# Even and odd tokens are put in order at y's eviction in two pieces per row instead of in the product, with a new order of all operations

## The chip, the cores and the metric

The kernel runs on 1 core of one Trainium2 chip. The metric is device time in microseconds; the time before is 193.65 us, the median of 3 runs (193.57 to 194.23). The core has five engines with a queue of instructions each: TensorE (PE in the profile; its weight loads are PEld), VectorE (DVE), ScalarE (ACT), GpSimd (POOL) and SyncE (SP). Here POOL and SP also issue nearly all the DMAs. Engines run their own queue in order and wait for each other by semaphores.

## What is computed

A gated linear recurrence for each of 4 batches and 8 heads, over 768 tokens with head size 48, and behind it a bilinear feed-forward over the 3072 tokens:

```python
state = np.zeros((B, H, D, D))                      # B, H, S, D = 4, 8, 768, 48
for t in range(S):
    state = alpha[:, :, t, :, None] * state + einsum('bhd,bhe->bhde', k[:, :, t], v[:, :, t])
    y[:, :, t] = einsum('bhd,bhde->bhe', q[:, :, t], state)
x = y.transpose(0, 2, 1, 3).reshape(B * S, H * D)   # 3072 x 384
out = ((x @ w_a) * (x @ w_b)) @ w_out               # 384 -> 1536 -> 384
```

Inputs and output are float32.

## The kernel before

**Chunks.** The work is cut into six chunks of 512 tokens: chunk c takes batches 0 and 1 (c even) or 2 and 3 (c odd), and of each of the two (called u = 0, 1, a "row") 256 tokens. A partition holds two neighbouring tokens, an even and an odd one (r = 0, 1), so all 256 tokens of a row are on 128 partitions, and each row falls into two halves of 128 tokens (g = 0, 1; partitions 0 to 63 and 64 to 127).

**An order written out by hand.** All operations stand in one string, `PROGRAM`. Each line begins with a chunk's number; then come operations with their arguments, separated by semicolons. They are called in this order, and each engine gets its instructions in that order; nothing is reordered later. A bank (0 to 7) in the arguments names the part of PSUM that an operation writes, a letter its engine: V for VectorE, S for ScalarE, P for GpSimd, Y for SyncE. The table OPS at the end maps names to functions. Those that matter here:

- `ld x u e` loads a, k, q or v (alpha, keys, queries, values) of a chunk; 0a and 0b are the two halves of the heads of u = 0. `W` and `Wo` load weights (POOL). They are DMAs, and POOL or SP spends about 0.5 to 1 us on issuing each.
- `c1a` calls for ScalarE's function table that has both the logarithm and the exponential. `cu`, `cus`, `ci`, `cm`, `cz`, `cs` and the like make constants; `fill` multiplies zeros.
- `ln` (la, line 556) takes the logarithm of alpha on ScalarE; `B`, `A2`, `AQ` sum it over tokens on TensorE; `ra` and `E` take exponentials on ScalarE.
- `mq` and `mk` (line 678) multiply q and k by these on VectorE into QKp; `C` transposes on TensorE and `Ce` evicts into kqT, or `T` transposes by DMA. `lv` prepares q and k of later chunks.
- `v` copies values into vx. `K`, `K2` and `k` carry the state over (Sm, S); `dk` and `de`, or `dr` and `dl`, bring its decay.
- `D` makes the scores on TensorE (line 841), masked by `M` (VectorE, line 846) or by `Mc` and `Mm` (ScalarE's copy, then VectorE in place).
- `SB`, `SA` and `Y` sum the row's output y in two banks of PSUM (line 865): 384 features in three groups of 128 partitions, for both halves g, 128 columns each, in which the 64 even tokens stand first and the 64 odd ones after them.
- `X u e` (`evac`, lines 900 and 902) evicts one row, 768 columns, into xT, the right-hand side of the feed-forward.
- `a` and `b` (`ff`, line 919) are the two first products of the feed-forward: for one of 12 groups f of 128 hidden features, three matmuls over the 384 inputs, for one row (0 or 1, 256 columns) or both (`*`, 512 columns). `as` (`ff_as`, line 925) evicts a on ScalarE, and `pr` (`ff_prod`, line 933) multiplies it on VectorE with b, which is still in PSUM, into prod.
- `o` and `oc` (lines 941 and 952) multiply prod by w_out, for 128 tokens m, in two halves of six groups; `ot`, `otc` evict and `st`, `stc` store.

**Where the even and odd tokens meet.** In xT each group of 128 tokens has the even ones first. `ff_prod` writes prod in token order: it reads a and b as (half, r, s) and writes every second element.

**How stages interleave.** The feed-forward of a chunk runs between the recurrence work of the next one. Chunk 0 has no other work to run beside it.

Of the kernel before, what the change touches and what calls it, by code (L numbers as in the profile page):

```python
# [50 lines left out]
1: ra 1
0: as 11 *
1: lv 0 q V; E 0 i
0: as 0 1; b 6 * 0; b 11 * 3; a 8 * 4; pr 6 *; pr 11 *
2: ld a * P
0: b 0 1 1; as 8 *; a 3 1 6
1: E 0 b; lv 0 k V
0: a 10 * 2; pr 0 1
1: mq 0 V; ld v 1 P
0: b 8 * 4  # L60
1: A2 1 7
0: as 10 *; b 10 * 2; pr 8 *
1: E 1 b
0: as 3 1; as 7 *; b 9 * 3; b 3 1 0; b 7 * 1; a 9 * 6
2: ld q * P
1: v 0 S; lv 1 q V; mk 0 V
0: pr 10 *
1: mq 1 V; C 0 1 4
0: as 9 *
1: C 0 0 2  # L70
0: o 0 0 5; pr 7 *
1: dk * 6
2: ld k * P
3: ld v * P
0: cz 1 v P; pr 9 *
1: Ce 0 0 S; E 1 i; de *; lv 1 k P; Ce 0 1 V; D 0 1 1; D 0 0 3
0: pr 3 1
1: Mc 0 0; K2 0 0 7 0
0: o 1 0 6
1: mk 1 V; M 0 1  # L80
0: o 3 0 4; o 1 1 -; ot 1 S; c3 P
3: ld a * P
0: cs 1 0 P; o 3 1 -
1: k 0 0 V; k 0 1 V; Mm 0 0 V; SB 0 1; C 1 0 3; C 1 1 7
0: ot 3 S; o 0 1 -
1: Ce 1 0 V
2: ln *
1: v 1 V; D 1 0 3; Ce 1 1 S; K2 1 1 6 0; Y 0; SA 0
0: ot 0 V
1: k 1 0 V; D 1 1 6  # L90
0: o 2 0 5
1: M 1 0
2: l2 0 V
1: X 0 S; a 3 0 1; Mc 1 1
2: l2s 0 P; l2s 1 P
1: a 2 0 3; a 4 0 4
2: R 0
1: k 1 1 V; as 4 0
2: ra 1
1: as 3 0; b 4 0 7  # L100
0: o 2 1 -
1: as 2 0
0: ot 2 S
1: pr 4 0
2: R 1; lv 1 q P
1: b 3 0 6; b 2 0 7; a 5 0 2; pr 3 0; b 5 0 3; as 5 0; b 1 0 5; a 1 0 1; pr 5 0; pr 2 0; a 7 0 2; as 1 0; pr 1 0
2: AQ 3
1: SB 1 6
2: lv 0 k P
1: a 10 0 5  # L110
2: lv 1 k V; ra 0; ld v * P
1: Mm 1 1 V
2: E 1 b
1: as 10 0; b 10 0 0; pr 10 0
2: mq 1 V; E 1 i
1: as 7 0; b 7 0 1
2: E 0 b; E 0 i
1: a 0 0 5
0: st 3 Y
2: dr  # L120
1: SA 1; Y 1
2: mk 1 V
1: pr 7 0; a 11 0 0; a 6 0 3; b 6 0 2; X 1 S; b 11 0 4; a 2 1 6; as 6 0; a 3 1 7; as 11 0; b 2 1 1; pr 6 0
2: lv 0 q V
1: b 4 1 0; as 2 1
2: T 1
1: pr 11 0
2: dl
0: st 0 Y
1: a 0 1 2; pr 2 1  # L130
2: mq 0 V
1: b 3 1 3; b 0 0 6; as 3 1; as 0 0; b 0 1 7; pr 3 1; a 8 0 1; a 9 0 5
0: st 1 Y
1: b 8 0 3; b 9 0 4; pr 0 0; as 0 1
2: mk 0 V
1: a 4 1 2
3: ln *
1: a 9 1 6; pr 0 1; as 8 0; b 9 1 1
3: ra 1
1: b 10 1 7; pr 8 0; a 10 1 3; as 4 1; as 9 0; as 9 1; a 6 1 6; b 6 1 2; b 11 1 5; pr 4 1; as 10 1; pr 9 0; a 11 1 4; pr 10 1; pr 9 1; as 6 1  # L140
2: v 1 S
1: a 8 1 3; b 8 1 1; a 7 1 6; pr 6 1
# [48 lines left out]
2: a 0 * 0; b 0 * 1; as 0 *; as 1 *
3: lv 0 k P; lv 0 q P
2: a 5 * 7
1: st 3 Y
2: a 7 * 4
4: l2s 1 P
2: a 2 * 5
3: lv 1 q V; mq 1 V; lv 1 k V
2: pr 1 *
3: dr  # L200
2: pr 0 *
3: mk 0 V
4: ld q * Y
0: st 2 Y
2: as 5 *; a 6 * 6; b 6 * 2; as 7 *
3: mq 0 V
2: b 9 * 4; b 7 * 0
1: st 2 Y
3: dl
4: R 0  # L210
2: b 5 * 7
1: o 1 0 3
2: a 9 * 1; pr 7 *; as 6 *
3: T 0
2: pr 6 *
4: ra 0
2: pr 5 *; a 11 * 6
3: mk 1 V
2: as 9 *; a 3 * 0
4: lv 0 k V; lv 0 q V; R 1  # L220
2: as 2 *
1: o 1 1 -
2: as 11 *; a 8 * 5; b 11 * 2; a 4 * 7; b 2 * 1
3: T 1
1: ot 1 V
2: pr 9 *; as 8 *; pr 11 *; pr 2 *; b 8 * 3; b 4 * 5; as 4 *
5: ld a * Y
3: K2 * * 4 6
2: pr 8 *; as 3 *; pr 4 *
3: k * 0 V; D 0 0 2; Mc 0 0  # L230
2: b 3 * 1
4: ra 1
2: pr 3 *; b 10 * 5; a 10 * 0
3: D 1 0 1; D 1 1 3
2: as 10 *
3: k * 1 V; Mc 1 1
2: o 0 0 7; o 2 0 0
3: M 1 0
# [860 lines left out]
```

## Time and profile before

The profiled execution has a span of 192.0 us, from the first to the last instruction; the three timed runs have a median of 193.65 us. The granted TensorE clock was 1.000 throughout. Some groups of the profile, by line and shape:

| what | engine | line | count | busy us | mean ns |
|---|---|---|---|---|---|
| a and b, 512 columns | PE | 919 | 324 | 82.2 | 379 |
| a and b, 256 columns | PE | 919 | 216 | 30.4 | 273 |
| o, 384 columns | PE | 941 | 276 | 49.4 | 326 |
| y, inner part | PE | 865 | 576 | 10.5 | 217 |
| eviction of y, 768 columns | ACT | 900 | 9 | 7.2 | 816 |
| eviction of y, 768 columns | DVE | 902 | 3 | 2.9 | 952 |
| eviction of the output, 384 columns | ACT | 956 | 15 | 7.4 | 492 |
| eviction of the output, 384 columns | DVE | 958 | 8 | 4.4 | 554 |
| masked scores, 1024 columns | DVE | 846 | 10 | 12.1 | 1220 |
| q, k products of chunk 0, 384 columns | DVE | 678 | 8 | 4.4 | 557 |
| load of the function table | ACT | 468 | 1 | 1.3 | 1283 |

A matmul's mean is its latency, since several are under way at a time; the time between two in a dense stretch is shorter. The products (line 933) stand singly in the profile, 0.73 us for 512 columns and 0.44 us for 256. The DMAs moved 29.4 MB in all.

### The profile page before, as it was taken

The page shows a single profiled execution, that of the slowest core. Times are in us where ns is not written, and L with a number is a line of the kernel's source. Part 1 is how long each engine was busy: PE and PEld are TensorE (multiplying, and loading weights), DVE is VectorE, ACT ScalarE, POOL GpSimd, SP SyncE. Part 2 cuts the span into 40 slices and gives each one's busy share as a digit, 9 for nine tenths or more (in the row PEclk, how much of TensorE's full clock was granted, in tenths as well). Part 3 has the DMA queues.
Part 4 walks back from the last instruction along what each step waited for, and adds up shares of the span by engine and source line. Part 5 has one row for each costly group of instructions (what it writes and reads, how often), then busy time and mean ns, then how long its engine had stood idle before and what let it go on. Part 6 is the DMA issues. An engine that isn't in the chain of part 4 may idle for free.

```text
span 192.0 us, 6086 instructions
## 1 busy us (share of the span) xinstructions
PE 186.8 (97%) x2613; PEld 116.9 (61%) x2613; DVE 133.1 (69%) x223; ACT 106.5 (55%) x194; POOL 56.9 (30%) x75
## 2 busy tenths in 40 slices
PE   7999999999999999999999999999999999999992
PEld 3888875677778876645557444656465644545562
DVE  2387698994989888899897956887567446252510
ACT  4448885656779867753487756743572435314211
POOL 8999626752450500640074262000000000000000
PEclk9999999999999999999999999999999999999999
DMA  5999999999969999999999989017641200000422
GB/s 132 274 219 218 251 253 235 244 269 264 251 107 166 165 216 265 248 254 149 233 213 181 156 174 129 3 42 140 146 66 44 85 0 0 0 0 3 164 82 82
DMA packets 62618, 29.40 MB, mean 153 GB/s; under 512 B 53712, under 2 KB 60768, under 8 KB 62592
## 3 DMA queue, kind: packets, MB, share of 16 engines
q0 software_dynamic: 18432, 13.37, 39.6%
q1 hardware_dynamic: 44016, 15.55, 38.1%
q8 instruction: 20, 0.33, 0.7%
q10 hardware_dynamic: 144, 0.10, 0.2%
q14 instruction: 6, 0.05, 0.1%
HBM read 25.98 MB, written 4.74 MB: 160 GB/s over the span
## 4 chain that ended last, share of the span: by engine, by line
PE 91%; DMA 5%; SPq 1%; DVE 1%; issue 1%; ACT 0%; DVEq 0%
PE psum L919 47%; PE psum L941 24%; PE psum L865 7%; PE psum L841 3%; DMA kqT<-QKp 3%; DMA q_t<-in_q_dram 3%; PE psum L736 2%; PE psum L633 1%; PE psum L952 1%; SPq L549 1%; PE psum L799 1%; PE psum L812 1%; PE psum L700 1%; PE psum L591 1%; PE psum L592 1%
## 5 line engine op out<-in xcount | busy, mean ns | idle before, releaser
L919 PE MATMUL psum<-xT,wb_t 128*128 128x512 bf16 (+1 forms) x270 | 56.0, 337 | 0.0
L919 PE MATMUL psum<-xT,wa_t 128*128 128x512 bf16 (+1 forms) x270 | 56.0, 337 | 0.0
L941 PE MATMUL psum<-wo_t,prod 128*128 128x384 bf16 x276 | 49.4, 326 | 0.0
L919 PEld LDWEIGHTS <-wb_t 128*128 128x128 bf16 x270 | 25.9, 98 | 19.9 <-issue 0.5
L919 PEld LDWEIGHTS <-wa_t 128*128 128x128 bf16 x270 | 25.9, 98 | 19.7 <-issue 0.3
L941 PEld LDWEIGHTS <-prod 128*128 128x128 bf16 x276 | 25.9, 98 | 17.6
L956 ACT ACTIVATE ot<-psum 128x384 f32<-128x384 f32 (+1 forms) x16 | 7.7, 482 | 22.7 <-PE psum L941 21.6
L850 ACT ACTIVATE m<-psum 128x1024 bf16<-128x1024 f32 x14 | 14.1, 1023 | 4.6 <-PE psum L841 4.3
L613 POOL TENSOR_TENSOR l<-la 64x384 f32<-64x384 f32 x7 | 7.8, 1108 | 26.6 <-ACT la L556 19.0
L846 DVE TENSOR_TENSOR m<-psum,mask 128x1024 bf16<-128x1024 f32 x10 | 12.1, 1220 | 3.1 <-PE psum L841 3.1
L652 POOL TENSOR_TENSOR q_t<-q_t,ra 128x384 f32<-128x384 f32 x5 | 6.1, 1215 | 22.5 <-ACT ra L645 19.7
L556 ACT ACTIVATE la<-a_t 128x1536 f32<-128x1536 f32 (+2 forms) x9 | 9.5, 1055 | 2.3 <-DMA a_t<-in_alpha_dram 2.2
L678 DVE TENSOR_TENSOR QKp<-q_t,beta 128x768 bf16<-128x768 f32 x10 | 10.0, 995 | 1.0 <-ACT beta L667 1.0
L865 PE MATMUL psum<-m,vx 64*64 64x128 bf16 x576 | 10.5, 217 | 0.0
L900 ACT ACTIVATE xT<-psum 128x768 bf16<-128x768 f32 x9 | 7.2, 816 | 5.7 <-PE psum L865 5.5
L678 DVE TENSOR_TENSOR QKp<-k_t,invb 128x768 bf16<-128x768 f32 x10 | 9.7, 972 | 0.8 <-ACT invb L667 0.8
L854 DVE TENSOR_TENSOR m<-m,mask 128x1024 bf16<-128x1024 bf16 x14 | 9.3, 684 | 1.2 <-ACT m L850 1.2
L958 DVE COPY ot<-psum 128x384 f32<-128x384 f32 (+1 forms) x9 | 4.8, 532 | 7.6 <-PE psum L941 4.7
L865 PEld LDWEIGHTS <-vx 64*64 64x64 bf16 x576 | 9.0, 107 | 0.5 <-issue 0.3
L841 PE MATMUL psum<-kqT 64*64 64x128 bf16 x384 | 9.0, 219 | 0.4 <-DMA kqT<-QKp 0.3
L652 POOL TENSOR_TENSOR k_t<-k_t,a_t 128x384 f32<-128x384 f32 x6 | 7.4, 1228 | 6.1 <-issue 3.3
L549 POOL DMA_DIRECT2D v_t<-in_v_dram x8 | 8.5, 1058 | 0.1
(271 smaller groups left out, 287.9 us busy)
## 6 DMA issues: line engine op xcount, KB each, us to landing
out_dram<-ot SPq DMA_DIRECT2D x23, 192.0 KB, 3.8
q_t<-in_q_dram SPq DMA_DIRECT2D x3, 768.0 KB, 6.5
a_t<-in_alpha_dram POOLq DMA_DIRECT2D x2, 768.0 KB, 15.2
k_t<-in_k_dram POOLq DMA_DIRECT2D x2, 768.0 KB, 12.1
v_t<-in_v_dram POOLq DMA_DIRECT2D x4, 384.0 KB, 7.0
a_t<-in_alpha_dram SPq DMA_DIRECT2D x2, 768.0 KB
k_t<-in_k_dram SPq DMA_DIRECT2D x2, 768.0 KB
a_t<-in_alpha_dram POOLq DMA_DIRECT2D x3, 384.0 KB, 8.5
```

The source lines that it names most:

```text
L549: eng.dma_start(out=t[:, us, hs].rearrange("p b h r d -> p (b h) (r d)"), in_=src[ch.b0 + us.start:ch.b0 + us.stop, hs, ch.s * 2 * C:(ch.s ...
L556: nc.scalar.activation(out=ch.la[:, us, hs].rearrange("p b h r d -> p (b h r d)"), in_=ch.a[:, us, hs].rearrange("p b h r d -> p (b h r d) ...
L613: eng.tensor_add(ch.l2[(1 - g) * HC:(2 - g) * HC, 1], x[:, :, 0, :], x[:, :, 1, :])
L652: eng.tensor_mul(x, x, by)
L678: eng.tensor_mul(QKp[ch.c % 2][:, u, j, :, hs, :D], src[:, u, hs].rearrange("p h r d -> p r h d"), f)
L841: nc.tensor.matmul(s2[g * HC:(g + 1) * HC, r, p, rk, :], lhsT=turned_part(ch, u, 1, rk, 2 * h + p, g, rs), rhs=queriesT(ch, u, 2 * h + p, ...
L846: nc.vector.tensor_mul(m.rearrange("p r a k s -> p (r a) (k s)"), ch.s2[u, h].rearrange("p r a k s -> p (r a) (k s)"), maskn(4))
L850: nc.scalar.activation(out=m.rearrange("p r a k s -> p (r a) (k s)"), in_=ch.s2[u, h].rearrange("p r a k s -> p (r a) (k s)"), func=AF.Copy)
L854: eng.tensor_mul(x, x, maskn(4))
L865: nc.tensor.matmul(y[c * DP:(c + 1) * DP, g, j // 2 * C:(j // 2 + 1) * C], lhsT=lhsT, rhs=rhs, start=(g, c) not in begun, stop=False, skip ...
L919: nc.tensor.matmul(p, lhsT=(wa_t, wb_t)[w][:, kk, f * 128:(f + 1) * 128], rhs=ch.xT[:, kk, us, :], start=(kk == 0), stop=(kk == KT - 1))
L941: nc.tensor.matmul(op, lhsT=ch.prod[:, f, at:at + C], rhs=wo_t[:, f, :], start=(f == 0), stop=(f == NFF - 1))
```

## The change

In the functions, three things change. `evac` takes one half g of a row at a time and puts the tokens in order as it writes xT; `ff_prod` multiplies without reordering; `tokens` and `columns`, which described the order there, are gone. `evict`, which existed before, copies on ScalarE or VectorE.

```diff
-    def evac(ch, u, eng):
+    def evac(ch, u, g, eng):
         if not hasattr(ch, "xT"):
             ch.xT = wk.tile([128, KT, B, C], BF16, name="xT")
-        o_ = ch.xT[:, :, 2 * u:2 * u + 2, :].rearrange("p a g s -> p g a s")
-        i_ = ch.y[u][0][:, :, :KT * C].rearrange("p g (a s) -> p g a s", a=KT)
-        if eng is nc.scalar:
-            nc.scalar.activation(out=o_, in_=i_, func=AF.Copy)
-        else:
-            eng.tensor_copy(o_, i_)
+        evict(ch.xT[:, :, 2 * u + g, :].rearrange("p a (s r) -> p a r s", r=2),
+              ch.y[u][0][:, g, :KT * C].rearrange("p (a r s) -> p a r s", a=KT, r=2), eng)
...
-        o_, a_, b_ = tokens(ch.prod[:, f, :], us), columns(a[:, :n], n), columns(b, n)
-        nc.vector.tensor_mul(o_, a_, b_)
+        nc.vector.tensor_mul(ch.prod[:, f, us.start * C:us.stop * C], a[:, :n], b)
...
-        "X": lambda x, u, e: evac(x, int(u), ENG[e]),
+        "X": lambda x, u, g, e: evac(x, int(u), int(g), ENG[e]),
```

`PROGRAM` is written anew from the first line to the last. Each operation on TensorE occurs as often as before, with the same shapes; its place and its bank change. Some operations change their engine: of the evictions of kqT, 4 of 8 are on ScalarE (2 before); of the v copies 4 of 12 (9 before); of the output evictions 14 of 25 with the `otc` (16 before); `lv` has 13 of 20 on GpSimd (11 before); `X` has 16 on ScalarE and 8 on VectorE (9 and 3 before). The beginning, up to chunk 0's first operation of the feed-forward, and the place of `c1a`:

```diff
-0: cm 0; c1; cz 0 b P; ci; ld a 0b Y; c1a; ld a 0a Y; ln 0b; cu; cz 1 b P; fill 7 2; cu2 V; cz 0 q V; cus; ld k 0b Y; ld k 0a Y; B 0b 5; ld q 0b Y; ld v 0 P
-0: ln 0a; ld q 0a Y; E 0b b; E 0b i; mq 0b V; B 0a 0; E 0a i; dk 0 2; E 0a b; ld a 1 P; mk 0b V; C 0 1 5; cs 0 m P; ld k 1 P; ld q 1 P; v 0 S; mk 0a V; cm 1
-0: de 0; fill 2 1; mq 0a V; C 0 0 3; Ce 0 1 V; W b 0 256; cz 0 v P; Ce 0 0 V; D 0 1 4; ln 1; ld v 1 P; W a 256 768; K 0 0 6; k 0 0 V; M 0 1; D 0 0 0; SB 0 6
-0: cz 1 q P; B 1a 2; M 0 0; W a 0 256; E 1a i; E 1a b; W b 256 768; mq 1a V; mk 1a V; B 1b 4; dk 1 3; E 1b i; E 1b b; de 1; v 1 S; mq 1b V; mk 1b V; C 1 0 0
-0: Y 0; SA 0; Ce 1 0 V; cs 1 m P
-1: ld a 0 P; ld a 1 P
-0: W a 768 1536; C 1 1 1; X 0 S; c2 P; D 1 0 3; W b 768 1536
...
-0: Ce 1 1 V; K 1 0 5; k 1 0 V; a 4 0 0
+0: ld a 0b Y; ld k 0b Y; ln 0b; c1; cz 0 q V; ld a 0a Y; ln 0a; ld a 1 P; ln 1; fill 7 0; cu; fill 2 1; cu2 V; cus; B 0b 2; ci; ld k 0a Y; ld v 1 P
+0: E 0b b; ld v 0 P; v 0 V; B 0a 0; B 1b 4; B 1a 6; E 0a i; mk 0a V; ld q 0a Y; E 0a b; E 0b i; mq 0a V; v 1 S; E 1b i; C 0 0 0; ld q 0b Y; mq 0b V; mk 0b V
+0: C 0 1 1; dk 0 2; K 0 0 3; E 1b b; ld k 1 P; mk 1b V; Ce 0 0 V; D 0 0 4; E 1a b; E 1a i; mk 1a V; ld q 1 P; Ce 0 1 S; D 0 1 0; mq 1a V; C 1 0 6; cz 0 b P
+1: ld a 0 P
+0: de 0; cs 0 m P; k 0 0 V; SB 0 2; cm 0; W a 256 768; cm 1; M 0 0; M 0 1; dk 1 7; de 1; mq 1b V; K 0 1 4; k 0 1 V; K 1 0 7; SA 0; W b 256 768; Ce 1 0 S
+0: k 1 0 V
+1: ln 0
+0: cz 0 v P; Y 0; X 0 0 V; D 1 0 0; K 1 1 5; C 1 1 4; Ce 1 1 V; k 1 1 V; c2 P; X 0 1 S; a 4 0 2; b 5 0 3; Mc 1 0; W a 0 256; as 4 0; b 4 0 0; pr 4 0; D 1 1 6
+0: Mc 1 1; SB 1 1
...
+0: cz 1 v P; Mm 1 0 V; b 3 0 4; a 5 0 0; as 5 0; a 0 0 5; a 3 0 6; Mm 1 1 V
...
+1: ln 1; H 0 V; L 0 V; ld k 0 P
+0: a 2 0 0; a 1 0 7; SA 1; Y 1; as 2 0; pr 5 0; as 3 0
+1: l2 1 V
+0: b 2 0 0; pr 2 0; X 1 1 S; cs 1 m P; X 1 0 S; W a 768 1536
+1: A2 0 6; ra 1
+0: b 0 0 2
...
+0: as 1 0
+1: ra 0
+0: b 3 1 3; W b 768 1536; a 2 1 0
+1: E 0 i; ld k 1 P; H 1 S
+0: pr 3 0; b 1 0 1; pr 1 0; as 0 0; pr 0 0; b 5 1 7; a 11 * 4; as 2 1; a 0 1 1; b 2 1 5; b 0 1 0
+1: E 0 b; L 1 V
+0: cz 1 q P; as 0 1; a 5 1 2; as 5 1
...
+0: pr 4 1; c1a
```

More of the change, by code (lines that the diff above doesn't have):

```diff
@@ L83 @@
[L83 to L106, printed above, removed]
@@ new lines @@
+2: l2s 0 P; R 0
+1: SB 1 0; X 0 1 V; D 1 0 3
+0: c3 P
+1: k 1 1 V
+0: o 3 1 -
+2: lv 1 k P
+0: ot 3 V
+1: a 3 0 6; b 4 0 5
+2: ra 1; R 1
+1: a 4 0 7
+0: o 1 0 2; o 1 1 -
+1: M 1 0; as 4 0; pr 4 0; as 3 0
+2: lv 1 q P
+1: a 5 0 3; as 5 0; b 5 0 4; Mm 1 1 V
+3: ld k * Y
+1: b 3 0 5; pr 5 0
+0: st 0 Y
+1: b 1 0 3
+0: ot 1 V
+2: AQ 6; E 0 i
+1: pr 3 0
+2: E 0 b
+1: Y 1; SA 1
+2: E 1 b
+1: X 1 1 S; X 1 0 V
+0: o 2 0 2
+1: a 1 0 6; b 8 0 0
+3: ln *
+1: a 8 0 1
+2: lv 0 k P
+0: o 2 1 -
+1: b 7 0 4
+2: mk 0 V; E 1 i; lv 0 q V; mq 0 V; mk 1 V
@@ new lines @@
+1: b 2 0 5
+0: ot 2 S
+1: a 2 0 7; a 10 0 2; as 8 0; pr 8 0
+2: mq 1 V
+1: b 10 0 1; as 1 0
+2: dr
+1: a 0 0 0; as 2 0; pr 2 0; pr 1 0
+2: T 0
+1: b 0 0 6
+2: T 1
+1: a 2 1 7; as 10 0
+3: lv 1 k P
+1: pr 10 0; a 7 0 2; as 0 0
+3: ld v * P
+1: pr 0 0; as 7 0; a 9 0 5
+3: lv 0 k V
+1: a 6 0 3; as 6 0; b 6 0 0; a 8 1 1; pr 7 0
+3: ra 1
+1: a 3 1 6; pr 6 0; b 8 1 2
+3: l2 0 V
+1: a 5 1 3
+3: l2s 0 V
+1: as 8 1; pr 8 1; as 9 0; as 3 1; b 9 0 0; pr 9 0; a 11 0 1; as 5 1; b 5 1 6; pr 5 1; a 1 1 4; as 1 1
@@ new lines @@
+2: v 1 S
+1: b 3 1 2; pr 3 1; b 11 0 0; b 0 1 3; b 1 1 6; pr 1 1
+0: st 1 Y
+1: b 10 1 2; as 11 0
+3: ra 0
+1: b 6 1 4; a 6 1 1; as 6 1
+0: cs 1 0 P
+3: l2s 1 P; R 0
+1: a 0 1 5; as 0 1; pr 11 0
+2: v 0 V
+5: ld a * Y
+3: R 1
+1: pr 6 1; o 2 0 6; a 10 1 0; as 10 1; pr 10 1; a 7 1 1; as 7 1; b 7 1 5; pr 0 1; pr 7 1; as 2 1; o 2 1 -
+2: D 1 1 0
+1: ot 2 S
+2: D 0 0 2; Mc 0 0
+4: ld a * Y; ln *
+1: b 2 1 4
+2: M 1 1
+1: o 0 0 5
+0: st 3 Y
+2: D 1 0 0; Mc 1 0; K2 * * 2 3
+1: a 9 1 6; as 9 1; a 11 1 7
@@ L208 @@
[L208 to L214, printed above, removed]
+3: mq 1 V; E 0 b; mk 1 V
+2: a 0 * 2
+4: l2s 0 P
+2: a 8 * 0
+3: mq 0 V; v 0 V
+2: as 8 *; pr 8 *; b 1 * 3; pr 1 *; a 4 * 4
+4: l2 0 V
+3: v 1 S
+2: b 10 * 0; b 7 * 5
+4: l2s 1 V
+3: mk 0 V; dr
+2: as 10 *; a 7 * 1; as 0 *; b 4 * 2
+3: T 1
+2: as 4 *; pr 4 *; pr 10 *; b 0 * 4; a 3 * 3
+4: ra 1
+2: pr 0 *
+4: R 0; ld v * P
+2: as 7 *
+5: ld v * P
+2: pr 7 *; a 9 * 2; as 9 *
+1: st 2 Y
+4: R 1
+2: b 9 * 0; pr 9 *; b 6 * 1; a 2 * 2
@@ L393 @@
[L393 to L400 removed]
+5: ln *
+1: st 0 Y
+2: o 0 0 1; o 0 1 -; ot 0 V
+3: SB 1 2; SB 0 6; Mm 0 0 V; D 0 1 4; Mc 0 1
+2: o 3 0 0; o 3 1 -; ot 3 S
+5: lv 0 k P
+2: st 3 Y
+3: Mm 0 1 V; Mm 1 1 V
@@ new lines @@
+4: AQ 4; E 1 b; E 1 i
+3: Y 0; Y 1; SA 1
+4: mq 1 V
+3: X 1 0 S
+5: l2 0 V; ld q * Y
+3: X 1 1 S; SA 0
+2: o 2 0 5; o 2 1 -
+4: E 0 b; dr
+1: st 1 Y
+4: lv 0 q V
+3: X 0 1 V; X 0 0 V; a 1 * 0
+4: lv 1 k P; mk 1 V; mq 0 V; E 0 i; mk 0 V
+3: a 2 * 1
+5: l2s 0 P; l2s 1 P; R 0; R 1
+3: a 5 * 4
+5: ra 0
+2: ot 2 S
+3: b 1 * 5; as 1 *; pr 1 *; a 6 * 0; as 6 *; b 2 * 2; a 0 * 3
+5: v 1 V
+3: as 2 *; b 6 * 0; pr 6 *; as 0 *; a 9 * 5; b 9 * 3; b 0 * 0; pr 2 *
+4: T 1
+3: as 9 *
+5: AQ 6
+3: as 5 *
+5: E 1 i
@@ new lines @@
+4: D 1 1 4
+5: E 0 i
+3: pr 9 *; pr 0 *
+5: E 0 b
+4: dl; K * 0 1; k * 0 V
+2: st 0 Y
+4: D 1 0 2; T 0
+5: E 1 b; lv 0 q V; mq 0 V; mk 0 V; T 0
+3: a 3 * 0; as 3 *; b 3 * 6; pr 3 *; b 5 * 1
+5: dr
+3: a 10 * 0
+4: Mc 1 1; Mm 1 1 V
+2: o 1 0 4
+4: Mc 1 0; Mm 1 0 V
+3: pr 5 *
+2: o 1 1 -; ot 1 S
+3: as 10 *; a 4 * 2; as 4 *
+5: ra 1
+3: a 11 * 3; as 11 *; b 4 * 0; pr 4 *; b 10 * 1; pr 10 *
+4: SB 0 4
+2: st 2 Y
+5: lv 1 q P
+4: D 0 0 6; M 0 0; SB 1 2
+3: a 7 * 0; o 2 0 1; as 7 *; a 8 * 0; as 8 *
@@ new lines @@
+4: D 0 1 6; SA 0
+5: v 0 V; mk 1 V
+4: M 0 1; SA 1; Y 1; X 1 0 S
+5: K * 0 0; dl; mq 1 V
+4: Y 0; X 0 0 S; X 0 1 V
+5: D 0 1 6
+3: b 7 * 2; pr 7 *
+5: M 0 1
+3: b 8 * 4
+4: X 1 1 S; a 0 * 5
+5: k * 0 V
+4: a 2 * 2
+3: pr 8 *; b 11 * 3; pr 11 *
+4: as 2 *; b 2 * 6
+2: st 1 Y
+4: pr 2 *; a 6 * 0; as 6 *; b 6 * 4; pr 6 *
+3: o 2 1 -; ot 2 V
+4: as 0 *
+3: o 0 0 2; o 0 1 -; ot 0 S
+5: T 1; D 1 1 0; Mc 1 1; D 1 0 4; M 1 0; SB 0 6; Mm 1 1 V
+3: o 3 0 2
+5: SB 1 0; D 0 0 4; Mc 0 0
+4: a 10 * 3; as 10 *
```

452 lines of the change are left out of this document (125 added, 327 removed).

## Prediction

> **What bounds the kernel now.** I read the page first (busy shares and slices), then the chain that ended last in order of time, then the timeline of all engines over the first 24 us, then the busy time in windows.
>
> ```profile
> span 192.0 us, 6086 instructions
> PE 186.8 (97%) x2613; PEld 116.9 (61%) x2613; DVE 133.1 (69%) x223; ACT 106.5 (55%) x194; POOL 56.9 (30%) x75
> PE   7999999999999999999999999999999999999992
> DMA  5999999999969999999999989017641200000422
> GB/s 132 274 219 218 251 253 235 244 269 264 251 107 166 165 216 265 248 254 149 233 213 181 156 174 129 3 42 140 146 66 44 85 0 0 0 0 3 164 82 82
> ```
>
> TensorE is the bound: only the first slice and the last show idle time. The DMA engines are saturated from about 2 us to 130 us. That matters only where TensorE waits for a load, which is in the first 18 us.
>
> ```profile
> 2.88 4.83 DMA q_t<-in_q_dram
> 18.39 0.43 PE psum L919 x3
> 57.47 9.93 PE psum L919 x90
> 79.14 7.77 PE psum L919 x36
> 182.77 0.49 PE psum L952 x6
> 188.69 0.33 ACT ot L956
> ```
>
> The chain holds a DMA and some DVE steps up to about 12 us, and after 18.39 us almost nothing but TensorE. Its pieces give prices that latency does not inflate. 7.77 us for 36 is 0.216 us for each 512-column matmul, and 9.93 for 90 is 0.110 us for each 256-column one. The one DMA piece late in the chain (kqT, at 106.47) cost TensorE only 0.3 us, by the list of waits. So the time is: 18.3 us until the feed-forward starts, 170.4 us of dense TensorE work, and 3.3 us of eviction and store after it.
>
> ```profile
> 0.73 1.28 ACT L468 ACT_TABLE_LOAD   x1 [0.73 <-PEq L1083]
> 3.62 1.14 ACT L556 ACTIVATE la<-a_t 128x384 f32<-128x384 f32 x2 [1.61 <-DMA a_t<-in_alpha_dram]
> 6.68 0.87 ACT L667 ACTIVATE prod<-psum 128x384 f32<-128x384 f32 x2 [1.92 <-PE psum L592]
> 7.81 0.56 DVE L678 TENSOR_TENSOR QKp<-q_t,prod 128x384 bf16<-128x384 f32 x1 [3.63 <-DMA q_t<-in_q_dram]
> 9.28 0.84 ACT L785 ACTIVATE vx<-v_t 128x768 bf16<-128x768 bf16 x1 [0.42 <-DMA v_t<-in_v_dram]
> 17.29 0.81 ACT L900 ACTIVATE xT<-psum 128x768 bf16<-128x768 f32 x1 [0.29 <-PE psum L865]
> 18.32 0.50 PE L919 MATMUL psum<-xT,wa_t 128*128 128x256 bf16 x3
> ```
>
> This is the start. There is one table load, under the wait for alpha. VectorE's first product starts at 7.81, when q has landed; the first v lands at 9.27 and only ScalarE waits for it; the first row's output leaves PSUM at 17.29 and the feed-forward starts at 18.32, 10.5 us after VectorE.
>
> **The change, part by part.** *TensorE's work.* Counting the operations of both lists: the same matmuls in the same shapes (chunk 1 and half of chunk 0 in 256 columns). The groups of 64x64 tiles that a 128x128 matmul follows are 23 where they were 25. Such a switch shows as 1.08 us instead of 0.98 for the next six output matmuls, so -0.2 us. No other term of the sum can come from TensorE's own work.
>
> *The product and the evictions.* 54 products of 0.731 us and 36 of 0.44 us now write in order. An unstrided row of the same kind with float32 in PSUM (m<-psum,mask, 1024 columns, 1220 ns) would put 512 columns at about 0.69, so the 90 products save 0 to 3 us of VectorE in all. The 12 evictions of 768 columns (9 x 0.816 on ACT, 3 x 0.95 on DVE) become 24 of 384 (16 on ACT, 8 on DVE), at the ot rows' 0.49 and 0.55: +0.5 and +1.5 us. Both lie under TensorE (DVE 69%, ACT 55%): 0 in the sum. Without that cover a row would cost 0.1 to 0.2 us more.
>
> *Table loads.* The preload (c1a) was the first thing on ACT; it now stands behind chunk 0's feed-forward. In the built program, loads come where a function is missing:
>
> ```
> 1 LoadActFuncSet
> 2,3,4 Activation la (0b, 0a, then all of u=1)
> 5 LoadActFuncSet
> 6 Activation prod<-psum
> 19 LoadActFuncSet        20 Activation la (chunk 1)
> 31 LoadActFuncSet        32 Activation ra (chunk 1)
> 51 LoadActFuncSet        (the moved preload)
> ```
>
> That is five loads instead of one, four of them where ACT has work behind them, at 1.28 us each by the row above.
>
> *The start.* ACT: alpha 0a is now third in SP's queue, and POOL's load of alpha u=1 shares the engines from the beginning. Before 0a are 0b and k 0b: 0.59 MB from SP, and about 0.4 MB from POOL by then. At 250 GB/s from 2.0 us that lands at about 6.0. Then la 0a 0.52, la u=1 0.85, load 1.28: the first exponential starts at 8.65 (before: 6.68), and the second, which VectorE's first product needs, ends at 9.5.
>
> VectorE: the v copy (0.35, the DVE row of vx<-v_t) now stands ahead of every product of chunk 0 and waits for v u=0, the third load on POOL, behind alpha u=1 and v u=1. POOL issues it at 3.9 (0.93 + 1.1 for ut and ident + 1.06, from 0.73 on). The shortest v load in the trace took 5.5 us from issue to landing: 9.4. By bytes: SP's six loads 1.18 MB, alpha 0.39, two v of 0.20, together 1.97 MB, and when v landed before, about 0.48 MB more had moved than stood ahead of it: 2.45 MB, which with 0.63 + 1.32 MB in the first two slices and 219 GB/s after is 11.9. I take the middle, 10.7, since both rows are of this queue. VectorE's first product: 10.7 + 0.35 = 11.05 (9.8 to 12.2).
>
> From there VectorE goes through this until the first row leaves PSUM: the eight products of q and k (8 x 0.55 = 4.4), kqT 0.69, state 0.36, two masks 2.44, state 0.71 + 0.36, eviction 0.55: 9.5 us. What is late behind the v wait is thus all of it, and TensorE's transposes, scores and inner products with it. On ACT the other half row (X 0 1) is queued behind kqT of u=1 (1.02), the Ln load (1.28) and la (0.85), and comes some 0.6 us after VectorE's half. Feed-forward starts at 11.05 + 9.5 + 0.6 = 21.15. It stands two state groups later in TensorE's order (K 0 1 and K 1 1, 0.25 us each), so it would be on par at 18.8: **+2.3 us** (9.8 + 9.5 + 0.1 gives +0.6; 12.2 + 9.5 + 0.6 gives +3.5).
>
> *The Exp load in the feed-forward.* Counting from the first feed-forward matmul: chunk 0's second output pair leaves PSUM on ACT at 5.4 (the masks free Y 1 at 3.4, two evictions follow). Then load 1.28, ra 0.52, as 1 0 0.38: bank 7 is free at 7.6. TensorE has 6.15 us of work until b 5 1 7, which writes that bank: 1.4 us of stall. The next, b 1 1 1, needs bank 1, behind ra, two exponentials, a copy and three as (3.1 us, 10.7), where TensorE comes at 9.9: 0.8 more. In the trace as evictions follow at 0.33 us though they last 0.38; over 12 instructions that gives back 0.5. **+1.7 us** (0.4 if the load is covered after all, 2.7 at most). The last load (c1a) is nearly idle time of ACT: 0, at most 0.5. The trace shows no ACT instruction right behind a load: 1.61 us lie between the end of the load and the first la, put down to a DMA. So what a load holds up behind it is between 0 and 1.6 us; I take 0, as the wait has an owner, and keep the other end.
>
> The Trainium skill, "ScalarE: Activation LUTs", section "What ACT_TABLE_LOAD costs", gives 1283 ns, as the trace has it, and a drain of some 1380 ns with every switch to another set, which no row here shows. By it the Ln and the Exp load would each cost that much more, and the sum would be about 2.8 us higher.
>
> *The rest of the order.* Transposes by DMA (5.1 us) are issued 5 us or more of TensorE work ahead of their scores in every chunk, as before; weights of columns 768 and up land near 26 us, just as a 11 wants them (0 to 0.5). I take 0, with -1.0 to +2. The tail has the same last pieces: 0.
>
> *Sum:* 2.3 + 1.7 - 0.2 = +3.8 on a span of 192.0: 195.8. The median of the runs lies 1.65 above the profiled span: **197.4 us**.
>
> **Rivals.** (1) *Faster: a denser middle.* From 18.39 to the last matmul the trace takes 170.3 us, and its matmuls at prices read off the chain in this way are 166.5; 2.5 of the 3.8 are the 25 switches, and 1.3 could go, besides the 0.2. It decides where the start is on par (v by 8.8, sooner than any v load here) and ACT's table loads are covered. Then 193.65 - 1.5 = 192.1. For it: ACT is 55% busy. Against it: TensorE has no visible idle time after 12 us, so there is little to win. 0.13.
>
> (2) *No change:* v lands early (first product at 9.8, +0.6) and ACT's loads are covered (+0.4), the rest -0.5: 194.1. 0.14.
>
> (3) *Loads that hold ACT longer,* up to the 1.6 us that the trace leaves open, at the two places where TensorE waits for ACT (X 0 1 and as 1 0): +3.2, 200.6. Its price by rows is an upper end. The skill's drain, cited above, is this rival. 0.2.
>
> (4) *The product is not cheaper* when it writes in order: as likely as not, and no time either way, while TensorE covers it.
>
> **How the numbers follow.** The forecast has 0.53. It ends at 197.4, its own range is 195.2 to 199.4. The range of 8 in 10 reaches to rival 2 below and most of the way to rival 3 above: 193.6 to 200.6. What this kernel's measurement can tell from no change is about 0.5%, 1 us. Faster by more: rival 1, 0.13. Within: rival 2, 0.14. Slower: the forecast and rival 3, 0.73.
>
> **What would show it.** Five table loads, the second at about 7.4 us and directly ahead of the first exponential; VectorE idle before the v copy, put down to the DMA of v, with products from about 11; the first feed-forward matmul near 21; TensorE waiting for as 1 0 some 6 us later, a load and ra ahead of it. If the feed-forward starts before 19, or TensorE is dense from there, the forecast is wrong.

## The result, and the profile after

The changed kernel takes **214.12 us** (213.17 to 215.12, 4 runs) against 193.85 us for the kernel before, run beside it: ratio 1.1043, 95% interval 1.1004 to 1.1081. Its profiled execution has a span of 212.2 us, 20.2 more than before. Some executions of a kernel take over 1.5% longer than its fastest; the times below leave those out, so that e3, e7 and e11 keep one execution each, and the profile of h3 is of one that is left out. From the page of the kernel after, the span, TensorE's busy time, and five rows in 40 slices of 5.3 us:

```profile
span 212.2 us, 6097 instructions
PE 195.5 (92%) x2613; PEld 123.4 (58%) x2613; DVE 137.4 (65%) x230; ACT 108.7 (51%) x201; POOL 60.5 (28%) x77
PE   7969998999898998999917998999999999999994
DVE  2076573899989997789817589888854244622342
PEclk9985599999999999999985999999999999999999
DMA  6999999999999998398994039835502010011023
GB/s 171 244 244 247 257 246 155 209 240 283 263 170 92 221 258 175 96 112 121 245 214 72 0 90 217 160 65 115 105 0 77 7 70 0 0 37 39 1 94 130
```

TensorE has the same 2613 matmul records in both, but is busy 8.7 us longer (195.5 less 186.8) and idle 11.5 us longer (16.7 less 5.2). The clock row shows two places where the granted clock halved, in slices 4 and 5 and in slices 21 and 22; just ahead of the second the PE row has its deepest hole. What TensorE waited for (releaser, then total us, times, longest us), from the list of waits:

```profile
PE psum L868 <- DVE prod L881: 6.9, 3, 6.0
PE psum L695 <- DVE QKp L637: 1.7, 2, 1.2
...
PE psum L868 <- ACT as__611 L874: 0.7, 1, 0.7
```

The first is the hole at 107 to 113 us, the second lies in the start, the third in the first feed-forward. Before, no wait behind the fillers of the start was longer than 0.3 us. The start, from the timelines of ScalarE, VectorE and TensorE (start, us, engine, line, operation, idle time before it):

```profile
3.43 0.52 ACT L515 ACTIVATE la<-a_t 128x384 f32<-128x384 f32 x1 [1.41 <-DMA a_t<-in_alpha_dram]
6.47 0.52 ACT L515 ACTIVATE la<-a_t 128x384 f32<-128x384 f32 x1 [2.51 <-DMA a_t<-in_alpha_dram]
7.50 0.84 ACT L515 ACTIVATE la<-a_t 128x768 f32<-128x768 f32 x1 [0.52 <-DMA a_t<-in_alpha_dram]
8.37 1.28 ACT L626 ACT_TABLE_LOAD   x1
9.66 1.64 ACT L626 ACTIVATE prod<-psum 128x384 f32<-128x384 f32 x4
...
11.67 0.36 DVE L746 COPY vx<-v_t 128x768 bf16<-128x768 bf16 x1 [8.29 <-DMA v_t<-in_v_dram]
...
12.56 0.86 PE L695 MATMUL psum<-ident,QKp 128*128 128x128 bf16 x8 [1.16 <-DVE QKp L637]
...
24.77 0.81 PE L868 MATMUL psum<-xT,wa_t 128*128 128x256 bf16 x3
```

The first exponential starts at 9.66 (6.68 before), VectorE's first product at 11.95 (7.81), the feed-forward at 24.77 (18.32). The largest single loss comes late. SP's queue, in order:

```profile
95.19 1.82 SPq L726 DMA_TRANSPOSE kqT<-QKp  x1
...
98.38 0.40 SPq L508 DMA_DIRECT2D q_t<-in_q_dram  x1
98.88 11.66 SPq L726 DMA_TRANSPOSE kqT<-QKp  x1
110.65 1.09 SPq L648 DMA_DIRECT2D bl<-row  x2
```

One transpose by DMA takes 1.82 us to issue; the next, behind a load of 0.79 MB on its queue and beside two more from POOL (issued at 96.5 and 99.2 us), takes 11.66, where the longest before was 3.27. The q that stands ahead of it lands 12.4 us after its issue, VectorE's step on it waits 5.5 us and starts at 110.78, and a product of the feed-forward is queued behind. The same stretch in windows (length, PE, PEld, DVE, ACT, POOL busy, granted clock, DMA share, GB/s):

```profile
104.00:106.00 2.00, 2.00 (x11) 0.88 (x9) 1.29 (x2) 0.99 (x2) 0.00 (x0) 1.00 1.28 291
...
108.00:110.00 2.00, 0.00 (x0) 0.00 (x0) 0.00 (x0) 0.00 (x0) 0.19 (x1) 0.87 1.67 210
110.00:112.00 2.00, 0.00 (x0) 0.00 (x0) 1.22 (x1) 0.00 (x0) 2.00 (x3) 0.50 0.94 201
112.00:114.00 2.00, 1.18 (x3) 0.25 (x2) 1.37 (x3) 0.60 (x1) 1.03 (x1) 0.50 0.69 101
```

From 108 us the compute engines stand still for almost 2 us, the DMA engines do not, and the clock halves while TensorE waits.

### The profile page after: what moved, and what is told of

The parts are those of the page before. It is cut to its first block, busy times and chain, and to the rows that moved or that the text cites. A ratio compares the mean times of both kernels' runs of the same rounds, so it can differ in the third digit from the quotient of the medians.

```text
span 212.2 us, 6097 instructions
## 1 busy us (share of the span) xinstructions
PE 195.5 (92%) x2613; PEld 123.4 (58%) x2613; DVE 137.4 (65%) x230; ACT 108.7 (51%) x201; POOL 60.5 (28%) x77
## 4 chain that ended last, share of the span: by engine, by line
PE 75%; DMA 9%; DVE 5%; issue 4%; ACT 3%; SPq 1%; POOL 1%; DVEq 0%; POOLq 0%; ACTq 0%
PE psum L868 37%; PE psum L889 20%; PE psum L824 7%; DMA q_t<-in_q_dram 6%; PE psum L800 4%; DMA v_t<-in_v_dram 3%; PE psum L695 2%; DVE QKp L637 2%; PE psum L659 2%; DVE prod L881 1%; PE psum L758 1%; PE psum L592 1%; ACT xT L904 1%; PE psum L771 1%; PE psum L900 1%
## 5 line engine op out<-in xcount | busy, mean ns | idle before, releaser
L868 PE MATMUL psum<-xT,wb_t 128*128 128x512 bf16 (+1 forms) x270 | 57.9, 343 | 8.1 <-DVE prod L881 6.0
L904 ACT ACTIVATE ot<-psum 128x384 f32<-128x384 f32 (+1 forms) x14 | 6.5, 467 | 16.7 <-PE psum L889 9.7
L611 POOL TENSOR_TENSOR k_t<-k_t,a_t 128x384 f32<-128x384 f32 x8 | 9.0, 1127 | 13.3 <-issue 9.5
L904 ACT ACTIVATE xT<-psum 128x384 bf16<-128x384 f32 x16 | 8.9, 604 | 6.5 <-PE psum L824 5.4
L906 DVE COPY ot<-psum 128x384 f32<-128x384 f32 x11 | 6.1, 555 | 9.3 <-PE psum L889 6.0
L800 PE MATMUL psum<-kqT 64*64 64x128 bf16 x384 | 11.0, 242 | 0.2 <-ACT as__1412 L874 0.2
L637 DVE TENSOR_TENSOR QKp<-k_t,invb 128x768 bf16<-128x768 f32 x10 | 11.1, 1108 | 0.0
L813 DVE TENSOR_TENSOR m<-m,mask 128x1024 bf16<-128x1024 bf16 x14 | 10.2, 738 | 1.2 <-ACT m L809 1.1
L746 DVE COPY vx<-v_t 128x768 bf16<-128x768 bf16 x8 | 4.9, 614 | 8.3 <-DMA v_t<-in_v_dram 8.3
L824 PEld LDWEIGHTS <-vx 64*64 64x64 bf16 x576 | 9.6, 112 | 1.0 <-issue 0.7
```

The source lines that it names most:

```text
L611: eng.tensor_mul(x, x, by)
L637: eng.tensor_mul(QKp[ch.c % 2][:, u, j, :, hs, :D], src[:, u, hs].rearrange("p h r d -> p r h d"), f)
L800: nc.tensor.matmul(s2[g * HC:(g + 1) * HC, r, p, rk, :], lhsT=turned_part(ch, u, 1, rk, 2 * h + p, g, rs), rhs=queriesT(ch, u, 2 * h + p, ...
L813: eng.tensor_mul(x, x, maskn(4))
L824: nc.tensor.matmul(y[c * DP:(c + 1) * DP, g, j // 2 * C:(j // 2 + 1) * C], lhsT=lhsT, rhs=rhs, start=(g, c) not in begun, stop=False, skip ...
L868: nc.tensor.matmul(p, lhsT=(wa_t, wb_t)[w][:, kk, f * 128:(f + 1) * 128], rhs=ch.xT[:, kk, us, :], start=(kk == 0), stop=(kk == KT - 1))
```

## Experiments

All times are medians; "one" marks a run that keeps one execution; each is set against the kernel before on the same chip (193.99 to 194.23 us).

| run | us | ratio, 95% interval |
|---|---|---|
| e6, order of before, new functions | 195.67 | 1.0065 [1.0043, 1.0088] |
| e15, the same, evictions on two engines | 196.94 | 1.0152 [1.0131, 1.0172] |
| e8, kernel before, nine table loads | 198.13 | 1.0213 [1.0171, 1.0254] |
| h1, new start, then order of before | 203.09 | 1.0450 [1.0421, 1.0478] |
| h4, new order to chunk 3, then before | 208.49 | 1.0733 [1.0701, 1.0765] |
| h3, order of before to chunk 3, then new | 208.38 | 1.0761 [1.0725, 1.0798] |
| e1, table first | 213.54 | 1.0997 [1.0955, 1.1038] |
| e2, gap filled | 213.35 | 1.0987 [1.0941, 1.1033] |
| e3, v behind products | 212.69 | one |
| e4, chunk 4's q step later | 214.21 | 1.1031 [1.0994, 1.1069] |
| e7, loads in the order of chunks | 218.78 | one |
| e9, e7 and e1 and e3 | 218.63 | 1.1275 [1.1215, 1.1335] |
| e10, loads behind the transpose | 207.73 | 1.0698 [1.0646, 1.0751] |
| e12, e10 and the gap filled | 209.64 | 1.0784 [1.0731, 1.0838] |
| e13, e10 and table first | 206.81 | 1.0620 [1.0577, 1.0663] |
| e11, e10 with all three of the start | 206.81 | one |
| e14, e10 with the start of before | 208.99 | 1.0761 [1.0728, 1.0794] |
| e16, e10, table, v, alpha in order | 205.50 | 1.0632 [1.0543, 1.0722] |

**The functions alone.** e6 has the order of before, with each `X u e` written as two:

```diff
-X 0 S
+X 0 0 S; X 0 1 S
```

> The order, banks and engines of before, with the new evac (each X split in two, on the same engine) and the new ff_prod. Theory 'the order costs it all': 193 to 194.5 us, span 191.5 to 193, five hundredths of the rise at most, one table load, granted clock 1.00. Rival 'the evictions in two pieces cost it': over 200 us, with TensorE waiting for xT.

195.67, above the theory's range and far below the rival's: the functions cost 1.6 us (195.67 less the 194.08 of the kernel before on the same chip; by the interval 0.8 to 1.7), the order the other 18. The products became cheaper (0.68 us for 512 columns, 0.73 before), but in the kernel after, the 24 evictions keep their engines busy for 13.5 us (8.9 for 16 of 0.604 on ScalarE, 4.6 for 8 of 0.588 on VectorE) where the 12 took 10.1. In e6 TensorE waits for them:

```profile
PE psum L915 <- ACT xT L951: 1.7, 2, 1.0
PE psum L736 <- DVE QKp L678: 0.8, 1, 0.8
```

e15 put the second of each pair on VectorE (`X 0 0 S; X 0 1 V`).

> The order of before with the new functions (195.7 us with a row's two evictions one behind the other on one engine, 1.05 us together), now with the first of them on ScalarE and the second on VectorE. Theory E (the 1.7 us are the longer way of y into xT, 0.81 us before): both take 0.6 us beside each other, TensorE's wait for xT falls from 1.7 us to under 0.5, 193.6 to 194.8 us. Rival (VectorE is busy at that point and the second eviction queues there, or the loss is elsewhere): 195.2 to 196.5.

A miss, above both ranges: 196.94. The wait moved to VectorE's queue:

```profile
PE psum L915 <- DVE xT L953: 1.8, 2, 1.3
```

**First tries at the start and at the late wait.** e1 moves `c1a` ahead of the first logarithm; e2 puts `fill 6` and `fill 3` ahead of `C 0 0` and `C 0 1`; e3 moves `v 0 V` behind chunk 0's first four products; e4 moves chunk 4's `lv 1 q V` to just ahead of its `AQ`.

> The changed kernel with c1a ahead of the first logarithm, nothing else: one table load instead of five. Theory (the loads stall TensorE as a recorded step of the prediction said, the v wait and the late q step stay): 2 to 3.5 us faster than the changed kernel, 210.6 to 212.1, no wait of TensorE for as and xT near 32 to 35 us, VectorE's first product still near 12. Rival 'ACT never mattered': within 0.7 us of 214.1.

> The changed kernel with six multiplications of zeros before C 0 0 and three before C 0 1, so that TensorE is busy while VectorE waits for v. Theory 'the clock fell because TensorE was idle from 11.4 us': granted clock 1.00 from 14 to 27 us where it was 0.50, first feed-forward matmul near 22.3 instead of 24.8, 3 to 5 us faster than the changed kernel (209 to 211). Rival 'the clock falls for another reason' or 'only the wait for v counts': clock still 0.50, within 1 us of 214.1 or slower.

> The changed kernel with VectorE's copy of v (v 0 V) behind the first four products of q and k instead of ahead of them. The start alone changes; the late wait stays. Theory 'the v wait starts the low clock': VectorE's first product near 10.3 instead of 11.95, first feed-forward matmul at 21.5 to 23 instead of 24.8, granted clock 1.00 there; the total within 2.5 us of 214.1, since the late wait takes most of it back. Rival 'v does not matter': first feed-forward matmul still past 24.3.

> The changed kernel with one operation of VectorE moved: chunk 4's q step (lv 1 q) stands just ahead of AQ 4 instead of among chunk 2's products. Theory 'VectorE waits there for q's load, and the products behind it hold TensorE's banks': the wait of 6 us at 107 us and the low clock behind it go, 6 to 8 us faster than the changed kernel (206 to 208). Rival 'q is late anyway and the wait only moves': within 2 us of 214.1, with the wait ahead of AQ 4 or of chunk 4's first scores.

None moved the end by more than 1.5 us. e1 did what it says at its place: chunk 1's first eviction comes at 52.6 us, 3.4 sooner than after's 56.0. But the logarithm of chunk 4's alpha, 1.48 us on ScalarE, starts only 0.9 us sooner, since it now waits for its load. Kernel after, then e1:

```profile
82.72 1.48 ACT L515 ACTIVATE la<-a_t 128x1536 f32<-128x1536 f32 x1 [1.68 <-DMA a_t<-in_alpha_dram]
```

```profile
81.81 1.48 ACT L515 ACTIVATE la<-a_t 128x1536 f32<-128x1536 f32 x1 [4.00 <-DMA a_t<-in_alpha_dram]
```

From there e1 stood before the same late wait (5.9 us). e2 kept the clock at 1.00 up to 22 us, and the feed-forward still started at 24.70: v landed 1.0 us later there (VectorE copies it at 12.71, not 11.67), and TensorE stood idle for 2.0 us at 20.4 to 22.4, with no releaser in the profile. e3 brought VectorE's first product from 11.95 to 11.27, where the second exponential ends, and the feed-forward to 23.13; but in its profile alpha 0a was logged at 7.80 in place of 6.47, so it does not show how far the start gains by this edit. All readings of the start have this limit, for its loads land at other times in each execution: in the profiles of the kernel after, e4, e7, e10, h1 and h4, which all have the changed start, alpha 0a is logged at 6.47 to 8.46 and the feed-forward starts at 24.0 to 25.9. In e4 the late wait came back under another name, 4.6 us for kqT, with the transpose still taking 11.56 us behind q's load.

**Loads in the order of the chunks.** In the changed order chunk 3's q is loaded ahead of chunk 2's, chunk 5's alpha ahead of chunk 4's, and chunk 4's q only beside the transpose. e7 turns these round; e9 adds e1 and e3.

> The changed kernel with the loads of q and alpha again in the order of the chunks: chunk 2's q before chunk 3's, chunk 4's alpha before chunk 5's, and chunk 4's q issued right behind its k. The two buffers of q and of alpha are handed out in the order of the loads, so in the changed kernel chunk 4's q waits until chunk 3's products are done and is issued at 98 us, 12 us before VectorE gets it. Theory 'this rotation is the late wait, and what the three single edits before this one gained was lost again in it': no wait for q's load and for chunk 4's alpha, no low clock near 110 us, 7 to 11 us faster than the changed kernel, 203 to 207. Rival 'the DMA engines are the bound there, whatever the order': within 2 us of 214.1.

> All three repairs: loads in the order of the chunks, the table loaded first (one load), VectorE's copy of v behind the products. Theory 'three separate losses, the first two hidden behind the third': 195 to 199, that is 3 to 8 us faster than with the loads alone in order. Rival 'the loads alone carry all': within 1.5 us of that kernel.

Misses by almost 12 us and more, and the most telling ones; e9 is as slow as e7, as its rival has it. In e7 chunk 4's q is issued at 82.9, well ahead of the transposes. But POOL's loads of chunk 5's v and k still fall beside the second transpose, and its scores wait. From the list of waits of e7, and from the timelines of POOL and SP:

```profile
PE psum L800 <- DMA kqT<-QKp: 10.7, 1, 10.7
```

```profile
96.73 1.15 POOL L508 DMA_DIRECT2D v_t<-in_v_dram  x1 [5.56 <-ACT vx L744]
99.38 1.15 POOL L508 DMA_DIRECT2D k_t<-in_k_dram  x1 [1.50 <-DVE QKp L637]
...
99.00 5.77 SPq L726 DMA_TRANSPOSE kqT<-QKp  x1
104.87 7.23 SPq L648 DMA_DIRECT2D bl<-row  x2
```

The scores start at 118.74, almost 20 us after the transpose was issued. So it is not the place of q in SP's queue, but the transpose in company with the loads. (Theory T.) One small load alone does not do it. In the kernel before, a transpose is issued together with a load of 0.39 MB on POOL, takes 3.27 us to issue, and TensorE does not wait for it:

```profile
112.00 3.27 SPq L767 DMA_TRANSPOSE kqT<-QKp  x1
```

```profile
112.04 1.19 POOL L549 DMA_DIRECT2D v_t<-in_v_dram  x1
```

**Theory T put to the test.** e10 lets the transpose run alone. `gatet` is an operation that the table already has: POOL copies one element of kqT, and so waits for the transpose. (Below, operations that share a line of the program stand apart.)

```diff
 2: as 7 *
-5: ld v * P
...
-4: ld q * Y
-4: lv 1 q V
-5: ld k * P
 3: Mc 0 0; dl
+4: ld q * Y
+3: gatet 0
+5: ld v * P; ld k * P
...
+4: lv 1 q V
 4: AQ 4; E 1 b; E 1 i
```

> The changed kernel with three loads of 0.4 to 0.8 MB put behind the last transpose by DMA of chunk 3: chunk 4's q (on SP, it stood one place ahead of the transpose) and chunk 5's v and k (on POOL, issued 96.5 and 99.2 us while the transpose of 98.9 us ran); POOL waits for the transpose before it issues them. Chunk 4's level step on q goes with its load. Nothing computed changes. Theory T (a transpose by DMA that is issued beside large loads takes 10 us and more instead of 2 to 5, and that is the 6 us for which TensorE stands at 107 to 113): the transpose lands within 5 us of its issue, the wait of 6 us for prod and the drop of the clock behind it are gone, 204 to 208 us. Rival (the wait only moves, to chunk 4's q or chunk 5's k, which now come later): 211 to 215.

207.73, as theory T has it: 6.4 us off. SP's queue and POOL's of e10:

```profile
97.20 3.02 SPq L725 DMA_TRANSPOSE kqT<-QKp  x1
...
101.84 0.18 POOL L940 CAST go<-kqT 1x1 f32<-1x1 bf16 x1 [12.61 <-DMA kqT<-QKp]
102.47 1.16 POOL L507 DMA_DIRECT2D v_t<-in_v_dram  x1 [0.46 <-ACT as__1936 L873]
```

The transpose lands 4.6 us after its issue, and TensorE is busy without a gap from 104 to 118 us, at a clock of 1.00.

**The order in pieces.** Both orders hold the same 852 operations (with each `X u e` written as two), so one can begin as one order and go on with what is left in the other, with some PSUM banks renumbered. h1 takes the changed order up to the last eviction before the feed-forward, h4 up to chunk 3's `AQ`, both then go on as before; h3 is h4 the other way round.

> The new functions with the changed order up to the last eviction ahead of the first feed-forward product, and from there the steps that are left in the order of before (a few PSUM banks renumbered where two steps would share one). Theory P (the loss is the sum of places, each keeps its own): 195.7 for the functions, and the 6 us by which the changed start comes late: 200 to 203. Rival (a late start is taken up later, as the early start of the run with the table load first was lost again): 196 to 198.5.

> The new functions with the changed order up to chunk 3's sum over tokens (AQ), then the steps that are left in the order of before. Theory P: 195.7 and the 10 to 12 us that the changed order is late at this step: 204 to 208. Rival (the late part of the order of before also stands behind loads that bunch, when it starts late): 210 to 214.

> The new functions with the order of before up to chunk 3's sum over tokens (AQ), then the steps that are left in the changed order. Theory P: 195.7 and the 7.5 us that the changed order loses between 95 and 115 us: 202 to 205. Rival (those 7.5 us come only because the work ahead ran late and the loads bunched): 196 to 199.

h1 and h4 are as the theory of places has them, 0.1 and 0.5 us above its ranges. From e6 by h1 and h4 to the kernel after the steps are 195.7, 203.1, 208.5, 214.1: **1.6 us for the functions, 7.4 for the start, 5.4 from there to chunk 3, 5.6 for the rest**; this last is what the transpose and the loads beside it cost (6.4 in e10). h3 misses upwards: by its profile, begun on time, the changed order waits for its own loads. Chunk 4's k is issued at 81.27 us, hardly sooner or later than in the kernel after (81.12); VectorE waits 4.7 us for it, and TensorE 5.4 us for an eviction queued behind. TensorE also waits 3.4 us for a transpose that was issued at 100.47 beside loads of q and k; its scores start at 112.83. These waits are a sign and no measure, since the profile is not of an execution in the table. In any case the parts don't add up from this side.

**The start, on e10.** With the late wait gone a gain ahead of it should stay.

> The kernel with the loads behind the transpose (207.7 us), with the combined table loaded first on ScalarE, v's copy behind the first four products with the decays on VectorE, and nine matmuls on zeros in TensorE's two gaps ahead of the first transposes. Theory S (the start loses by ScalarE's table loads, 3 us and more, and by the clock that halves behind the gaps, some 3 us, and with the late wait gone a gain of the start stays): 200.5 to 203.5. Rival (the start's loss is the order of loads and products itself): 205 to 208.

> The kernel with the loads behind the transpose (207.7 us), with the nine matmuls on zeros alone. Theory S: the clock stays at 1.00 up to 22 us, and the end comes 2 to 4 us earlier, 203.7 to 205.7. Rival (TensorE waits for VectorE and ScalarE there whatever its clock): 206.8 to 208.6.

> The kernel with the loads behind the transpose (207.7 us), with the combined table loaded first alone: one table load in place of five. Theory S: the 3.3 us that the same edit gained up to chunk 2's sum in the changed kernel now stay, 203.5 to 205. Rival (something else behind it takes them up): 206.5 to 208.

> The order of before up to the last eviction ahead of the first feed-forward product, then the steps that are left in the changed order with the loads behind the transpose (207.7 us with the changed start). By places: 207.7 less the 7.4 us of the start, 199.5 to 201.5. Rival (the changed order behind the start loses its time whatever comes ahead, as the order of before did not): 203 to 207.

None reaches what its theory said. Filling the gaps gains nothing (e12: 1.9 us slower than e10, with intervals that just overlap). The table load alone gives 0.9 us (e13), inside the two intervals, and the three together the same 0.9 in one execution (e11). e14 is no clean test: the changed order behind the seam wants weights (1.4 us of wait) and ScalarE (3.4 us) at other moments than the start of before leaves them, and the second row is evicted at 33.4 us instead of 23.8.

e16 last takes away the place that held up e1, by loading chunk 4's alpha ahead of chunk 5's, with the edits of e1 and e3, on e10.

> The kernel with the loads behind the transpose (207.7 us), with the combined table first and v's copy behind the first four products (together they bring chunk 2 forward by 2.5 to 3.4 us), and with chunk 4's alpha loaded ahead of chunk 5's. Theory C (a gain of the start is lost where the pace is set by a load: at chunk 4's alpha, and at the transposes; both are gone): chunk 4's log starts by 79, the gain stays, 203 to 205. Rival (a third place takes it up, or chunk 5 now wants its alpha): 206 to 209.

At its place it does what it should; chunk 4's logarithm waits for nothing:

```profile
79.19 1.48 ACT L515 ACTIVATE la<-a_t 128x1536 f32<-128x1536 f32 x1
```

The end gains 2.2 us on e10 by the medians, less than the intervals can tell, and lies between the theory's range and the rival's, so it decides neither; another 2.5 us of wait for an eviction (VectorE, xT) stands ahead of chunk 3's feed-forward. No kernel here is faster than the one before.

**Table loads in the order of before.** e8 moves `c1a` of the kernel before behind chunk 0's feed-forward, so that ScalarE loads nine times.

> The kernel before with c1a moved behind chunk 0's pr 8, nothing else: nine table loads instead of one, eight of them in a kernel whose TensorE is dense. Theory by the row (1.28 us each, two or three of them in the start where TensorE waits for ACT, the others partly covered): 3 to 6 us slower than before, 197 to 200. Theory with a wait behind each load of another 1.4 us: 6 to 11 us slower. Rival 'ACT covers them': within 1 us of before.

198.13, as expected: 3.9 us for eight more loads, 0.5 us each. ScalarE's timeline there:

```profile
3.58 1.18 ACT L556 ACTIVATE la<-a_t 128x384 f32<-128x384 f32 x2 [1.57 <-DMA a_t<-in_alpha_dram]
4.78 1.28 ACT L667 ACT_TABLE_LOAD   x1
6.09 0.87 ACT L667 ACTIVATE prod<-psum 128x384 f32<-128x384 f32 x2
```

## Why the prediction was right and wrong

Slower was right; 197.4 was 16.7 us short, and 214.1 lies outside the range. By its own steps:

- **The step "The rest of the order", taken at 0, failed by about 11 us** (5.4 and 5.6 by the pieces). Its ground was that transposes by DMA are issued 5 us or more ahead of their scores, at 5.1 us each. The lead was there; the duration was not. 5.1 us is what a transpose takes in the order of before. The changed order puts three loads beside one of them, whose issue alone then took 11.66 us; e10, which keeps the loads back, shows that they did it. The step looked at when a transfer is issued and not at what runs beside it. The 5.4 us of the middle are placed, not explained; chunk 4's alpha, logged 1.9 us sooner in e16 than in e10, may be one part of them.
- **The start: +2.3 was mis-sized; the run of it alone gives 7.4.** The single pieces were near: alpha 0a logged at 6.47 for 6.0 (in this execution; 7.6 to 8.5 in the five other profiles of this start), first exponential at 9.66 for 8.65, first product at 11.95 for 11.05 (inside 9.8 to 12.2), held by v as it said (the second exponential ended at 10.5). From there to the feed-forward it forecast 10.1 us and 12.8 passed. The sum has VectorE busy without a gap; it waited 2.9 us for TensorE, whose clock stood at 0.50:

```profile
17.09 0.36 DVE L785 TENSOR_TENSOR Sm<-psum,bl 128x192 bf16<-128x192 f32 x1 [1.09 <-PE psum L758]
...
21.23 0.36 DVE L788 TENSOR_TENSOR tmp<-psum,Sm 128x192 f32<-128x192 f32 x1 [0.89 <-PE psum L758]
...
23.18 0.59 DVE L906 CAST xT<-psum 128x384 bf16<-128x384 f32 x1 [0.93 <-PE psum L824]
```

In the profile of e10, with the same start, the clock stood at 1.00 up to 21 us and the first two of these waits are gone, but the third is 2.12 us, for TensorE had idled 1.91 us without a releaser; the feed-forward started at 24.01. So a kept clock alone gives little (e2, e12). How the 7.4 us divide stays open; e1, with one table load, has chunk 1's first eviction 3.4 us sooner, but the end of e13 hardly moves.
- **The Exp load in the feed-forward: +1.7.** The mechanism is right, and at the named place: TensorE waits 0.75 us for as 1 0, and 0.40 for a product behind it, 1.15 for the forecast 1.7; with the table first (e13) these are at most 0.25.
- **The product and the evictions: 0 in the sum.** Wrong by 1.6 us. Evictions were priced by the output rows (0.49 and 0.55) and took 0.60 and 0.59; and they are not covered by TensorE's work where a row's second half is what the next products wait for (e6).
- **No further loads, tail 0:** the tail holds; five table loads came, where they were said to.
- **Rivals.** The denser middle and no change fall with 214.1 us. The longer hold of ScalarE falls too: behind a load the next instruction starts at once, 0.01 us later in the kernel after (9.66) and 0.03 in e8 (6.09). The Trainium skill, "ScalarE: Activation LUTs", "What ACT_TABLE_LOAD costs", names a drain of some 1380 ns at each switch beside the load; these rows show none. Eight more switches cost 3.9 us of time in e8; by the Trainium skill's figures they would take ScalarE an estimated 21 us. That the product is not cheaper was wrong: 0.68 for 0.73.

## What to carry to other kernels

Price a DMA by what runs beside it, not by its median: ask of each moved load which transposes and which other loads it now meets. A gain ahead of a place where a load sets the pace can be lost there (e1), so take away the last wait first and measure the earlier edits on that. Look at several profiles of the same start before a difference of 1 us in it is put down to an edit. Where an order is written anew as a whole, run pieces of the two orders joined at seams; it places the loss in a few runs, as long as the seam itself brings no wait.

## What was not expected of the hardware

- A transpose by DMA landed 4.6 us after its issue alone (e10), and about 20 us after it beside two loads of 1.2 MB together (e7), while the page of e7 shows 97, 119 and 77 GB/s in the three slices from 103 to 119 us, where plain loads move some 250. The loads suffer too: that k took 18 us to land. Which of the loads, or how many bytes, it takes was not measured. The Trainium skill, "Advanced Engine Details and Errata", "X-Bar Transpose (TRN2)", has transposes as fast as regular DMAs; here that holds for one that runs alone (0.39 MB in 4.6 us; a load of v as large, alone at 88 us in e10, took 5.6).
- The granted clock fell to 0.50 after two gaps of 1.16 and 0.54 us of TensorE at 11.4 to 14.0 us, and came back only at 27.6, nearly 3 us after the first large matmuls; in e10, with gaps of 0.48 and 0.63 us at the same place, it stayed at 1.00, and fell at 21.4 behind 1.9 us of idle time. In h1 it fell behind a gap of 1.88 us at 7 to 9 us, in e10 not behind one of 2.02 at the same point. The steps of the clock in the kernel after come at 7.1, 13.9, 27.6, 109.5 and 116.3 us, which is 2, 4, 24 and 2 times 3.41 us apart; so it may count where a gap lies between two such points. No run tests that.
- An eviction that writes every second element took 0.60 us on ScalarE for 384 columns, against 0.49 for the output rows, which are as long.
- Up to 2.3 us of TensorE's idle time near 20 us (e4; 1.9 in e10, none in the kernel after) has no releaser in the profile. In both traces a packet of 16 KB of the instruction queue (q8 on the page) starts 0.4 to 0.5 us before TensorE stops (at 20.13 in e4, 18.74 in e10), so it may wait for its instructions; no run tests it.
